# Loading w_out behind the first batch's keys, with the linear product as a third piece and the key work moved back in group 0's turn

## The chip, the cores and the metric

One core of one Trainium2 chip. The metric is the device time of one execution in microseconds (us), taken as the median of several executions. All runs told here are of the fast state. The span in a profile is about 1.8 us shorter than the time of the same execution (in six executions with fillers, told below, 2.0 to 2.5). The mean granted clock of an execution is the share of TensorE's full clock that it got on average, 1.000 being all of it.

## The reference, cut to what matters

Agent attention, then a feed-forward layer that takes the larger of three products:

```python
# q, k, v: (4, 12544, 128); agents: (4, 49, 128); w1, w2, w3: (128, 768); w_out: (768, 128)
a2k = softmax(scale * agents @ k.T);  agent_v = a2k @ v          # over all keys of a batch
q2a = softmax(scale * q @ agents.T);  x = q2a @ agent_v
h = maximum(maximum(x @ w1, x @ w2), x @ w3)
out = h @ w_out
```

The kernel folds `agent_v` into the weights. For each batch it forms G, 49 rows of agents against all weight columns. With w3-w1, w2-w1 and w1 in place of w1, w2, w3, the larger of three becomes w1 plus a second slice against a rectified first one, and the w1 part goes through w_out at once as a linear product of 128 columns ("the linear part", columns C1O to WC of G).

## The kernel before: the parts that matter

Work is queued with a key by `at(key, function, name, needs, ...)`; the keys are sorted, and what still lacks its needs or a PSUM buffer waits and goes as soon as it can. The result is one fixed program per engine. Queries come in 49 groups of 1024 rows. A group has six slices of 128 columns, each a "first" (`u`), a rectification on ScalarE (`a`), a "second" (`v`) and a maximum on VectorE (`x`); slice 3 does both on ScalarE. In the turn of query group s the keys of the next batch are worked off as key tile s. Ahead of group 0 stands a stage for all of batch 0's keys and values.

```python
    def load_weights():                       # queued behind the loads of four key groups
        for t, w in zip(wst, (moe_w1, moe_w2, moe_w3)):
            nc.sync.dma_start(t, w)
        nc.sync.dma_start(wo_st, moe_w_out.rearrange("(f p) d -> p f d", p=P))
    ...
    def prep_weights():                       # in the key stage
        nc.scalar.activation(w1_bf, wst[0], AF.Copy)
        nc.scalar.activation(wo_bf, wo_st, AF.Copy)
    ...
    def prep_linear1():                       # in the key stage, first_key + 43
        t = small_tile("o_ps")
        for f in range(NF):
            nc.tensor.matmul(t[:, :C], w1T[:, f, :], wo_bf[:, f, :], start=(f == 0), stop=(f == NF - 1))
        nc.scalar.activation(wall[:, C1O + C:C1O + 2 * C], t[:, :C], AF.Copy)
    ...
    def keep_busy(times):                     # filler matmuls
        t = small_tile("m_ps")
        for _ in range(times):
            nc.tensor.matmul(t, ident, busy, start=True, stop=True, skip_group_check=True)
```

PSUM holds three large buffers ("uv") and two small ones ("om").

The softmax here doesn't subtract the row's maximum and nothing guards it: scores larger than these inputs give would overflow.

Of the kernel before, what the change touches and what calls it, by code (L numbers as in the profile page):

```python
# [11 lines left out]
AF = mybir.ActivationFunctionType  # L12
# [4 lines left out]
def kernel(  # L17
# [18 lines left out]
    nc = tc.nc  # L36
# [81 lines left out]
    def at(key, fn, name=None, needs=(), ring=None, frees=()):  # L118



        ops.append((key, len(ops), fn, name, needs, ring, frees))
# [53 lines left out]
    wo_st = const.tile([P, NF, C], FP32, name="wo_st")  # L176
# [4 lines left out]
    def load_weights():  # L181
        for t, w in zip(wst, (moe_w1, moe_w2, moe_w3)):
            nc.sync.dma_start(t, w)
        nc.sync.dma_start(wo_st, moe_w_out.rearrange("(f p) d -> p f d", p=P))

    ag_bf = const.tile([A, B, C], BF16, name="ag_bf")
    wo_bf = const.tile([P, NF, C], BF16, name="wo_bf")
# [3 lines left out]
    C21, C31, C1O = 0, Dff, 2 * Dff  # L191
    wall = const.tile([P, 2 * Dff + 3 * C], BF16, name="wall")
    nc.vector.memset(wall[:, C1O:], 0.0)
    WC = 2 * Dff + 2 * C
# [8 lines left out]

    def prep_weights():
        nc.scalar.activation(w1_bf, wst[0], AF.Copy)
        nc.scalar.activation(wo_bf, wo_st, AF.Copy)
        fi = slice(FI * P, (FI + 1) * P)
        nc.vector.tensor_tensor(out=wall[:, C21:C21 + Dff], in0=wst[1], in1=wst[0], op=ALU.subtract)
        nc.vector.tensor_tensor(out=wall[:, C31:C31 + Dff], in0=wst[2], in1=wst[0], op=ALU.subtract)
        nc.vector.tensor_tensor(out=wall[:, C31 + FI * P:C31 + (FI + 1) * P], in0=wst[2][:, fi],  # L210
                                in1=wst[1][:, fi], op=ALU.subtract)

    def prep_linear0():
        t = small_tile("m_ps", BF16)
# [23 lines left out]
    def k_group(b, t0, n, key, s):  # L238
# [3 lines left out]
        K = None if early else table(s)  # L242
# [75 lines left out]
        if early:  # L318
            g = ("early", t0)
            at(key - 30, load)  # L320
            at(key - 5, cast_k)
            at(key - 4, cast_v)
            at(key, turn_k, ("kt", g), (), "uv", [("kt_out", g)])
            at(key + 0.5, evacuate, ("kt_out", g), [("kt", g)])

            last = [("normalise", 0)] if t0 + n == NT else []
            late = max(0, (key - last_key) / 6 + 2)
            at(min(key + 6.6, last_key + 0.58 + 0.02 * late), scores, ("ks", g), [("kt_out", g)],
               "uv", [("ka", g)] + last)
            at(min(key + 7, last_key + 0.64 + 0.01 * late), exps, ("ke", g), [("ks", g)])  # L330
            done = last_key + (0.6 + 0.1 * late if late >= 1 else 0.55)
            at(min(key + 13.2, done), values, ("kv", g), [("ke", g)])
            at(min(key + 13.6, done + 0.01), add_values, ("ka", g), [("kv", g)])
        else:
            at(key - 24.6, load)
            at(max(key - 12.6, last_key - 3.4 + 0.2 * s), cast_k, ("k_cast", s))
            at(max(key - 10.6, last_key - 3.3 + 0.2 * s), cast_v, ("v_cast", s))
            if s > 1:
                at(max(key - 9.1, last_key - 3.2), turn_k, ("kt_out", s), [("k_cast", s)])
            else:  # L340

                turn = 1.2 if s else last_key + 1.05
                at(turn, turn_k, ("kt", s), (), "uv", [("kt_out", s)])
                at(turn + 0.05, evacuate, ("kt_out", s), [("kt", s)])

            at(key + K["ks"] if s else K["u0"] + 0.6, scores, ("ks", s), [("kt_out", s), ("ho", s)])
            at(key + K["ke"], exps, ("ke", s), [("ks", s)])
            at(key + K["ke"] + 1.5, add_exps, ("kx", s), [("ke", s)])
            at(key + K["kv"], values, ("kv", s), [("ke", s), ("v_cast", s)])
            at(key + K["ka"], add_values, ("ka", s), [("kv", s)])  # L350

    def k_tail(b, sum_key, keys, s):
        d = {}

        def reduce():
            d["e"] = work.tile([P, A], FP32, tag="e_sum", name="e_sum")
            nc.vector.tensor_reduce(out=d["e"], in_=Eacc[b].rearrange("p (j a) -> p a j", a=A),
                                    axis=mybir.AxisListType.X, op=ALU.add)

        def total():  # L360
            d["s"] = host[s]
            nc.tensor.matmul(host[s][:, :A], ones, d["e"], start=True, stop=True,
                             skip_group_check=True)

        def normalise():

            r = (last_tile["t"] if s is None else d["s"])[:, :A]
            nc.vector.reciprocal(r, Vacc[b][:, A:] if s is None else r)
            d["avT"] = work.tile([P, H], BF16, tag="avT", name="avT")
            nc.vector.memset(d["avT"][:, A:], 0.0)  # L370
            nc.vector.tensor_tensor(out=d["avT"][:, :A], in0=Vacc[b][:, :A], in1=r, op=ALU.mult)
            G[b] = work.tile([P, WC], BF16, tag="G", name="G")

        def product(c0, c1, on_vector):
            t = uv_tile()
            cuts = [c for c in range(c0, c1, 512)] + [c1]
            for i, (a, z) in enumerate(zip(cuts, cuts[1:])):
                for lo, hi in ((a, min(z, C1O)), (max(a, C1O), z)):
                    for h in range(2 if lo < hi else 0):


                        c = lo + (C if lo >= C1O and h == 0 else 0)
                        nc.tensor.matmul(t[h * H:(h + 1) * H, i, lo - a:hi - a], d["avT"],  # L383
                                         wall[:, c:c + hi - lo], start=True, stop=True,
                                         skip_group_check=True)
            src = t.rearrange("p i c -> p (i c)")[:, :c1 - c0]
            if on_vector:
                nc.vector.tensor_copy(out=G[b][:, c0:c1], in_=src)
            else:
                nc.scalar.activation(G[b][:, c0:c1], src, AF.Copy)  # L390

        if s is not None:
            at(sum_key - 1, reduce, ("sum_e", b), [("kx", s - 1)])
            at(sum_key, total, ("total", s), [("sum_e", b), ("ho", s)])
        at(sum_key + (0.9 if s is None else 0.01), normalise, ("normalise", b),
           [("ka", ("early", NT - last_size)) if s is None else ("total", s)])
        for i, (c0, c1) in enumerate(((C31, WC), (C21, C31))):
            on_vector = s is None and i == 0
            at(keys[i], lambda c0=c0, c1=c1, on_vector=on_vector: product(c0, c1, on_vector),
               ("product", b, i), [("normalise", b)], "uv", [("product", b, i)])  # L400


    def split(t0, t1, step):
# [10 lines left out]
    def q_group(s):  # L414
# [3 lines left out]
        key = 6.0 * s  # L418
# [36 lines left out]
        K = table(s)  # L455
# [63 lines left out]
        def out_linear(o):  # L519
            t = d["o", o] = small_tile("o_ps")  # L520
            for i, jj in enumerate(pairs[o]):
                nc.tensor.matmul(t[:, i * 2 * C:(i + 1) * 2 * C], d["e"][:, jj * P:(jj + 1) * P],  # L522
                                 G[batch[jj]][:, C1O:C1O + 2 * C], start=(i == 0), stop=False,
                                 skip_group_check=True)
# [20 lines left out]
                nc.sync.dma_start(out[r0:r1, :].rearrange("(p j) c -> p j c", j=m), src)  # L545

        new = [("product", tails[s], i) for i in range(2)] if s in tails else []

        def put(name, fn, *needs, ring=None, frees=()):
            at(key + K[name], fn, (name, s), needs, ring, frees)  # L550
# [23 lines left out]
        if s:  # L574
            put("ho", host_tile, ring="om", frees=[("rec", s)] + extra)
        else:
            at(K["u0"] - 0.04, host_tile, ("ho", 0), (), "om", [("rec", 0)] + extra)
        put("sum", sums, ("ex", s), ("ho", s),
            *([("ks", s)] if s in hosting else [("total", s)] if s + 1 in tails else []))
        put("rec", recips, ("sum", s))  # L580
# [10 lines left out]
            put(x, each(max_second), (v, s), (a, s),  # L591
                *([(f"oc{o}{f}", s - 2) for o in range(2)] if s >= 2 else []))
        for o in range(2):
            put(f"lin{o}", lambda o=o: out_linear(o), ("ex", s), *new, ring="om", frees=[(f"sc{o}", s)])
            for f in range(NF):
                put(f"oc{o}{f}", lambda o=o, f=f: out_hidden(o, f), (f"lin{o}", s), (f"x{f}", s))
            put(f"sc{o}", lambda o=o: out_scale(o), ("rec", s),
                *[(f"oc{o}{f}", s) for f in range(NF)], *([("store", s - 3)] if s >= 3 else []))
# [23 lines left out]
    at(first_key - 6.5, load_weights)  # L622
    at(first_key + 30.2, prep_weights)
    at(first_key + 37.1, prep_linear0, "lin_a", (), "om", ["lin_a"])
    at(first_key + 43, prep_linear1, "lin_b", ["lin_a"], "om", ["lin_b"])
    fillers = []
    for g, n in enumerate(first_sizes):
        k_group(0, sum(first_sizes[:g]), n, first_key + 6.0 * g, None)

        if 4 <= g < len(first_sizes) - 5:  # L630
            fillers += [(first_key + 6.0 * g + 0.55, 3), (first_key + 6.0 * g + 1.3, 3)]
    k_tail(0, last_key, (last_key + 0.95, last_key + 1.02), None)
    for key, n in fillers + [(last_key + 0.9, 2), (last_key + 1.1, 2),
                             (KEY["u1"] + 0.61, 2)]:
        at(key, lambda n=n: keep_busy(n), ("busy", key), (), "om", [("busy", key)])
# [45 lines left out]
```

## Time and profile before

| | |
|---|---|
| time, median | 466.05 us (465.85 to 466.12, 3 runs) |
| span of the profiled execution | 465.3 us |
| TensorE, VectorE, ScalarE, GpSimd busy | 94%, 87%, 85%, 36% |
| stage of batch 0's keys | until about 42 us, DMA share 0.98 at 380 GB/s |
| TensorE without a gap | from about 57 us |

The prediction below shows the lines and reads them. One thing about this profile was seen only later: its execution is one of the longer ones. Its time was 467.13 us, 1.1 above the median, and the cast of key tile 0 starts at 44.40 us. In a profile of a kernel that has the same program up to there (`b_keys`, below) it starts at

```profile
43.12 1.15 POOL L252 CAST k_bf<-st 128x1152 bf16<-128x1152 f32 x1 [0.48 <-DMA st<-in_k_dram]
```

and spans of the kernel before in later runs are mostly 464.2 us. A delay of about 1.1 us in the loads of the key stage thus lies in the profile of before and not in the timed runs. So moments are compared below by their distance from the start of key tile 0's cast.

### The profile page before, as it was taken

The page shows a single profiled execution, that of the slowest core. Times are in us where ns is not written, and L with a number is a line of the kernel's source. Part 1 is how long each engine was busy: PE and PEld are TensorE (multiplying, and loading weights), DVE is VectorE, ACT ScalarE, POOL GpSimd, SP SyncE. Part 2 cuts the span into 40 slices and gives each one's busy share as a digit, 9 for nine tenths or more (in the row PEclk, how much of TensorE's full clock was granted, in tenths as well). Part 3 has the DMA queues.
Part 4 walks back from the last instruction along what each step waited for, and adds up shares of the span by engine and source line. Part 5 has one row for each costly group of instructions (what it writes and reads, how often), then busy time and mean ns, then how long its engine had stood idle before and what let it go on. Part 6 is the DMA issues. An engine that isn't in the chain of part 4 may idle for free.

```text
span 465.3 us, 13301 instructions
## 1 busy us (share of the span) xinstructions
PE 436.1 (94%) x5452; PEld 274.3 (59%) x5456; DVE 405.6 (87%) x516; ACT 396.6 (85%) x461; POOL 166.6 (36%) x166
## 2 busy tenths in 40 slices
PE   2496899999999999999999999999999999999996
PEld 2365466666655766666656666666656555555554
DVE  3164699999998999999999999999998989999995
ACT  3366889989989999899889898998999989999992
POOL 2244864553550544535262446353230100100000
PEclk9999999999999999999999999999999999999999
DMA  8999999998998999997997999997746557553222
GB/s 320 394 412 404 409 270 378 298 347 227 297 310 276 279 273 333 314 273 214 271 345 261 279 323 309 275 272 191 176 114 194 147 169 174 160 136 114 69 86 97
DMA packets 82632, 118.53 MB, mean 255 GB/s; under 512 B 56391, under 2 KB 57867, under 8 KB 82571
## 3 DMA queue, kind: packets, MB, share of 16 engines
q1 hardware_dynamic: 82368, 117.59, 83.5%
q8 instruction: 42, 0.69, 0.6%
q14 instruction: 19, 0.16, 0.1%
q10 hardware_dynamic: 203, 0.10, 0.1%
HBM read 78.74 MB, written 25.69 MB: 224 GB/s over the span
## 4 chain that ended last, share of the span: by engine, by line
PE 77%; ACT 6%; issue 3%; DVE 3%; ACTq 0%; DVEq 0%
PE uv_ps L492 33%; PE o_ps L531 28%; PE o_ps L522 5%; ACT a_sb L507 4%; PE m_ps L446 4%; PE m_ps L466 3%; DVE r L517 2%; PE m_ps L295 2%; PE m_ps L284 1%; PE m_ps L480 1%; ACT uv_ps L504 1%; ACT e_q L472 1%; PE uv_ps L383 1%; PE o_ps L613 0%; ACT G L390 0%
## 5 line engine op out<-in xcount | busy, mean ns | idle before, releaser
L517 DVE TENSOR_TENSOR r<-uv_ps,a_sb 128x1024 bf16<-128x1024 f32 x245 | 297.4, 1220 | 15.6 <-PE uv_ps L492 5.9
L507 ACT ACTIVATE a_sb<-uv_ps 128x1024 bf16<-128x1024 f32 x245 | 240.6, 1027 | 13.2 <-PE uv_ps L492 11.7
L492 PE MATMUL uv_ps<-e_q,G 49*128 49x512 bf16 (+3 forms) x1248 | 186.3, 368 | 2.2 <-DVE r L517 0.6
L531 PE MATMUL o_ps<-wo_bf,r 128*128 128x128 bf16 x2352 | 174.7, 220 | 0.2 <-DVE r L517 0.2
L531 PEld LDWEIGHTS <-r 128*128 128x128 bf16 x2352 | 137.8, 98 | 39.8 <-issue 37.9
L492 PEld LDWEIGHTS <-G 49*128 49x128 bf16 x1248 | 57.9, 93 | 63.4 <-issue 31.1
L312 POOL TENSOR_TENSOR Eacc<-Eacc,e_k 128x441 f32<-128x441 f32 (+1 forms) x30 | 30.5, 1016 | 129.8 <-ACT e_k L289 129.8
L538 DVE TENSOR_TENSOR o_sb<-o_ps,recips 128x512 f32<-128x512 f32 x98 | 67.5, 689 | 9.4 <-PE o_ps L531 6.5
L441 POOL CAST q_bf<-st 128x1024 bf16<-128x1024 f32 x49 | 51.0, 1043 | 63.1 <-DMA qT<-q_bf 61.8
L515 ACT ACTIVATE r<-uv_ps 128x1024 bf16<-128x1024 f32 x49 | 50.2, 1024 | 21.8 <-PE uv_ps L492 21.7
L252 POOL CAST k_bf<-st 128x1152 bf16<-128x1152 f32 (+2 forms) x45 | 51.0, 1132 | 28.8 <-DMA st<-in_k_dram 27.1
L504 ACT ACTIVATE uv_ps<-uv_ps 128x1024 f32<-128x1024 f32 x49 | 49.5, 1011 | 1.0 <-ACT a_sb L507 0.7
L522 PE MATMUL o_ps<-G,e_q 128*128 128x256 bf16 x196 | 38.0, 276 | 0.0
L259 POOL CAST v_bf<-st 128x1152 bf16<-128x1152 f32 (+1 forms) x33 | 37.5, 1137 | 0.6 <-DMA st<-in_v_dram 0.3
L472 ACT ACTIVATE e_q<-m_ps 128x512 bf16<-128x512 f32 x49 | 29.8, 609 | 0.5 <-PE m_ps L466 0.5
L257 ACT ACTIVATE v_bf<-st 128x1152 bf16<-128x1152 f32 (+1 forms) x12 | 12.9, 1072 | 16.1 <-DMA st<-in_v_dram 16.1
L272 DVE COPY kT<-uv_ps 128x1152 bf16<-128x1152 bf16 (+1 forms) x14 | 9.9, 708 | 17.5 <-PE uv_ps L266 17.4
L522 PEld LDWEIGHTS <-e_q 128*128 128x128 bf16 x196 | 12.5, 97 | 18.5 <-issue 17.8
L266 PE MATMUL uv_ps<-ident,k_bf 128*128 128x128 bf16 x116 | 11.2, 254 | 12.3 <-POOL k_bf L252 11.8
L446 PEld LDWEIGHTS <-q_bf 128*128 128x128 bf16 x264 | 14.8, 98 | 13.1 <-issue 11.5
L451 DVE COPY qT<-m_ps 128x1024 bf16<-128x1024 bf16 x32 | 21.8, 680 | 0.0
L446 PE MATMUL m_ps<-ident,q_bf 128*128 128x128 bf16 x264 | 20.4, 220 | 0.3 <-POOL q_bf L441 0.3
(68 smaller groups left out, 233.4 us busy)
## 6 DMA issues: line engine op xcount, KB each, us to landing
st<-in_q_dram SPq DMA_DIRECT2D x46, 512.0 KB, 5.3
out_dram<-o_sb SPq DMA_DIRECT2D x46, 512.0 KB, 3.8
st<-in_k_dram SPq DMA_DIRECT2D x40, 576.0 KB, 7.0
st<-in_v_dram SPq DMA_DIRECT2D x40, 576.0 KB, 7.5
st<-in_k_dram SPq DMA_DIRECT2D x3, 512.0 KB, 6.9
st<-in_v_dram SPq DMA_DIRECT2D x3, 512.0 KB, 6.1
wst<-in_moe_w_dram SPq DMA_DIRECT2D x3, 384.0 KB, 10.8
st<-in_q_dram SPq DMA_DIRECT2D x2, 384.0 KB, 4.7
```

The source lines that it names most:

```text
L252: nc.gpsimd.tensor_copy(out=d["kb"][:, :n, :], in_=d["k"][:, :n, :])
L259: nc.gpsimd.tensor_copy(out=d["vb"][:, :n, :], in_=d["v"][:, :n, :])
L441: nc.gpsimd.tensor_copy(out=d["qb"], in_=d["q"])
L446: nc.tensor.transpose(t[:, j * P:(j + 1) * P], d["qb"][:, j, :], ident)
L492: nc.tensor.matmul(t[:, h, j0 * P:j1 * P], G[b][h * H:h * H + A, col + f * P:col + (f + 1) * P], d["e"][h * H:h * H + A, j0 * P:j1 * P], s ...
L504: nc.scalar.activation(u, u, AF.Relu)
L507: nc.scalar.activation(a_sb[f], u, AF.Relu)
L515: nc.scalar.activation(r, v_ps[f], AF.Relu)
L517: nc.vector.tensor_tensor(out=r, in0=v_ps[f], in1=a_sb[f], op=ALU.max)
L522: nc.tensor.matmul(t[:, i * 2 * C:(i + 1) * 2 * C], d["e"][:, jj * P:(jj + 1) * P], G[batch[jj]][:, C1O:C1O + 2 * C], start=(i == 0), stop ...
L531: nc.tensor.matmul(t[:, c:c + C], r_sb[f][:, h, jj * P:(jj + 1) * P], wo_bf[:, f, :], start=False, stop=True, skip_group_check=True)
L538: nc.vector.tensor_tensor(out=d["out"][:, j:j + m, :], in0=d["o", o].rearrange("p (j c) -> p j c", c=C), in1=d["r"][:, j:j + m].unsqueeze( ...
```

## The change

Its intent: w_out isn't needed until the first outputs, so its 393 KB should not hold up the keys that group 0 waits for; the linear part, which needs w_out, then has to follow in group 0's turn; and group 0's own key work, whose tile comes no sooner, moves behind the first slices. Cut to its core:

```diff
     def load_weights():
         for t, w in zip(wst, (moe_w1, moe_w2, moe_w3)):
             nc.sync.dma_start(t, w)
+
+    def load_w_out():
         nc.sync.dma_start(wo_st, ...)
...
         nc.scalar.activation(w1_bf, wst[0], AF.Copy)
-        nc.scalar.activation(wo_bf, wo_st, AF.Copy)
...
+    def prep_w_out():
+        nc.gpsimd.tensor_copy(out=wo_bf, in_=wo_st)
...
-            at(key + K["ks"] if s else K["u0"] + 0.6, scores, ...)
+            at(key + K["ks"] if s else 0.26, scores, ...)
...
-        for i, (c0, c1) in enumerate(((C31, WC), (C21, C31))):
+        pieces = ((C31, C1O), (C21, C31), (C1O, WC)) if s is None else ((C31, WC), (C21, C31))
+        for i, (c0, c1) in enumerate(pieces):
...
-            at(K["u0"] - 0.04, host_tile, ("ho", 0), ...)
+            at(0.25, host_tile, ("ho", 0), ...)
...
-    at(first_key + 43, prep_linear1, "lin_b", ["lin_a"], "om", ["lin_b"])
+    at(last_key - 29.85, load_w_out)
+    at(last_key - 3.28, prep_w_out)
+    at(1.9, prep_linear1, "lin_b", ["lin_a"], "om", ["lin_b"])
...
-    k_tail(0, last_key, (last_key + 0.95, last_key + 1.02), None)
+    k_tail(0, last_key, (last_key + 0.95, last_key + 1.02, 2.4), None)
```

More of the change, by code (lines that the diff above doesn't have):

```diff
@@ L344, in k_group @@
                 at(turn + 0.05, evacuate, ("kt_out", s), [("kt", s)])
-            at(key + K["ks"] if s else K["u0"] + 0.6, scores, ("ks", s), [("kt_out", s), ("ho", s)])
+            at(key + K["ks"] if s else 0.26, scores, ("ks", s), [("kt_out", s), ("ho", s)])
             at(key + K["ke"], exps, ("ke", s), [("ks", s)])
@@ L396, in k_tail @@
            [("ka", ("early", NT - last_size)) if s is None else ("total", s)])
-        for i, (c0, c1) in enumerate(((C31, WC), (C21, C31))):
+        pieces = ((C31, C1O), (C21, C31), (C1O, WC)) if s is None else ((C31, WC), (C21, C31))
+        for i, (c0, c1) in enumerate(pieces):
             on_vector = s is None and i == 0
             at(keys[i], lambda c0=c0, c1=c1, on_vector=on_vector: product(c0, c1, on_vector),
-               ("product", b, i), [("normalise", b)], "uv", [("product", b, i)])
+               ("product", b, i), [("normalise", b)] + ["lin_b"] * (i == 2), "uv", [("product", b, i)])
     def split(t0, t1, step):
@@ L547, in q_group @@
         new = [("product", tails[s], i) for i in range(2)] if s in tails else []
+        new_linear = new if s else [("product", 0, 2)]
         def put(name, fn, *needs, ring=None, frees=()):
@@ L576, in q_group @@
         else:
-            at(K["u0"] - 0.04, host_tile, ("ho", 0), (), "om", [("rec", 0)] + extra)
+            at(0.25, host_tile, ("ho", 0), (), "om", [("rec", 0)] + extra)
         put("sum", sums, ("ex", s), ("ho", s),
@@ L593, in q_group @@
         for o in range(2):
-            put(f"lin{o}", lambda o=o: out_linear(o), ("ex", s), *new, ring="om", frees=[(f"sc{o}", s)])
+            put(f"lin{o}", lambda o=o: out_linear(o), ("ex", s), *new_linear, ring="om",
+                frees=[(f"sc{o}", s)])
             for f in range(NF):
```

## The prediction

> **What bounds the kernel now.** I read the page first, then busy time by stretches, then the chain of waits, then what GpSimd (POOL) and ScalarE (ACT) did between 42 and 57 us.
>
> ```profile
> PE 436.1 (94%) x5452; PEld 274.3 (59%) x5456; DVE 405.6 (87%) x516; ACT 396.6 (85%) x461; POOL 166.6 (36%) x166
> ```
> TensorE is busy for 94% of the span, so the question is where the missing 6% lies. The stretches answer it.
>
> ```profile
> 0.00:42.00 42.00, 22.70 (x386) 18.91 (x389) 16.21 (x37) 20.24 (x26) 13.98 (x18) 1.00 0.98 380
> 42.00:47.40 5.40, 4.79 (x76) 3.02 (x74) 3.46 (x9) 3.05 (x6) 3.74 (x4) 1.00 1.02 408
> 47.40:53.90 6.50, 5.07 (x60) 2.83 (x61) 3.57 (x7) 4.38 (x7) 5.24 (x6) 1.00 1.02 409
> 53.90:57.30 3.40, 3.18 (x27) 1.12 (x26) 2.80 (x3) 3.40 (x6) 3.02 (x4) 1.00 1.03 410
> ...
> 65.60:132.00 66.40, 66.40 (x860) 42.28 (x860) 63.66 (x81) 60.63 (x72) 31.10 (x30) 1.00 1.05 309
> ```
> Columns: stretch, length, busy us of PE, weight load, DVE, ACT, POOL, then granted clock, DMA share, GB/s. Until 42 us the core waits for batch 0's keys and values: DMA is full at about 410 GB/s. From 57 us on PE has no gap. So the change can act only on the start, up to about 57 us; every microsecond that PE's dense run begins sooner or later comes out at the end almost 1:1, because nothing behind it has slack.
>
> GpSimd casts what lands, in order:
> ```profile
> 42.88 1.04 POOL L441 CAST q_bf<-st 128x1024 bf16<-128x1024 f32 x1 [1.25 <-DMA st<-in_q_dram]
> 44.40 1.15 POOL L252 CAST k_bf<-st 128x1152 bf16<-128x1152 f32 x1 [0.49 <-DMA st<-in_k_dram]
> 45.81 1.15 POOL L259 CAST v_bf<-st 128x1152 bf16<-128x1152 f32 x1 [0.26 <-PE uv_ps L383]
> 47.00 1.04 POOL L441 CAST q_bf<-st 128x1024 bf16<-128x1024 f32 x1
> 48.50 1.15 POOL L252 CAST k_bf<-st 128x1152 bf16<-128x1152 f32 x1 [0.46 <-DMA st<-in_k_dram]
> ```
> These are group 0's queries, group 0's keys and values, group 1's queries and keys. Between 44 and 48 us GpSimd has nearly no room: query tile 1 is cast the moment value tile 0 is done.
>
> ScalarE in group 0's turn:
> ```profile
> 46.64 0.80 ACT L390 ACTIVATE G<-uv_ps 128x768 bf16<-128x768 f32 x1
> 47.84 1.02 ACT L507 ACTIVATE a_sb<-uv_ps 128x1024 bf16<-128x1024 f32 x1 [0.39 <-PE uv_ps L492]
> 48.76 0.54 ACT L289 ACTIVATE e_k<-m_ps 128x441 bf16<-128x441 f32 x1
> 49.18 1.03 ACT L507 ACTIVATE a_sb<-uv_ps 128x1024 bf16<-128x1024 f32 x1
> 50.88 1.01 ACT L504 ACTIVATE uv_ps<-uv_ps 128x1024 f32<-128x1024 f32 x1 [0.67 <-ACT a_sb L507]
> 52.94 1.02 ACT L515 ACTIVATE r<-uv_ps 128x1024 bf16<-128x1024 f32 x1 [1.05 <-PE uv_ps L492]
> 53.86 1.98 ACT L507 ACTIVATE a_sb<-uv_ps 128x1024 bf16<-128x1024 f32 x2
> ```
> I call these G1, a0, key exps, a1, relu of slice 3, second relu of slice 3, then a2 and a4. The gaps of 0.67 and 1.05 us are waits for slices. The chain of waits runs through the last two:
> ```profile
> 53.86 1.99 ACT a_sb L507 x2
> 55.85 0.04 issue
> 55.90 0.39 PE uv_ps L492 x2
> 56.29 0.32 PE o_ps L613
> ```
> From 55.90 on the chain is PE after PE. So the hand-over from "ACT sets the pace" to "PE sets the pace" is the end of a4 at 55.85 us. That is the point to compute after the change.
>
> [...] PE idles 1.00 us at 48.35 before the key values' product (it waits for the key exps) although slices 0 and 3, next in program order, need nothing from it. So order in the program is what this change trades in. [...] ScalarE here shows 278 ns for 128 columns and 1027 for 1024, so about 0.84 ns a column and 0.17 us fixed. Cutting one evacuation into two is therefore paid for.
>
> **The change part by part.**
>
> *w_out's load moves behind query tile 0.* 768x128 floats are 393 KB, at 410 GB/s 0.96 us. Batch 0's keys, its values from the fifth group on, and query tile 0 land 0.96 us sooner. All that comes behind (key tile 0 and later) has the same bytes ahead of it as before, so it lands when it did: key tile 0 still at 44.40.
>
> *Product in three pieces.* The first evacuation on DVE, 1024 columns in 1.23 us, becomes 768 columns, about 0.95; two matmuls fewer ahead. Slices can start from the first two pieces; query tile 0's exps (46.15 to 46.75 before, now 0.96 sooner) and G1 (now 45.7 to 46.5) are ready in time.
>
> *Start of the slices.* The transposes of key tile 0 stand ahead of slice 0 on PE. They started at 46.37, after PE's earlier work, with slice 0 1.04 us later at 47.41. Now they wait for the cast that ends at 44.40 + 1.15 = 45.55, so they start at 45.60 and slice 0 at 46.64. Gain 0.77, not 0.96. a0 then runs 47.07 to 48.09.
>
> *w_out's cast on GpSimd.* 1152 columns take 1.15 and 512 take 0.62 us, so 768 take about 0.83. By its key it comes between value tile 0 and query tile 1: 47.00 to 47.83. Query tile 1's cast moves to 47.85 to 48.90 (before 47.00 to 48.04).
>
> *Key work behind the first slices.* New PE order: slices 0, 1, two fillers, second slice 0, slice 3, then query tile 1's transposes (key 0.222), then key tile 0's scores (0.26). The second slice 0 and slice 3 are done by 48.4 (slice 3 needs a0's buffer, 48.09). But query tile 1's transposes stand ahead of the scores and now wait until 48.95; they take 0.46, so scores start at 49.41 (before 47.95). Key exps still stand ahead of a1 on ACT: they run at 49.9 (before 48.76), ACT idling from 48.09 to 49.9. Then a1 ends at 51.3 (before 50.2) and slice 3's first relu at 52.25 (before 51.9; it loses less because its slice is ready and the gap of 0.67 is gone). On PE the key values' product follows the exps at 50.5 and the sums at 50.7; reciprocals and the first maximum follow at about 51.25 to 51.5 on DVE (before 50.97). Then second slices 1 and 3 run about 52.5 to 53.05, against 52.24 to 52.86. So this reordering eats the 0.77 gained and about 0.2 more.
>
> *Linear part in group 0's turn.* Its two parts had cost nothing on the path in the DMA stage:
> ```profile
> L206 ACT ACTIVATE wo_bf<-wo_st 128x768 bf16<-128x768 f32 x1 | 0.8, 827 | 0.0
> ...
> L223 ACT ACTIVATE wall<-o_ps 128x128 bf16<-128x128 f32 x1 | 0.3, 278 | 0.9 <-PE o_ps L222 0.9
> ```
> Now six matmuls (key 1.9) follow second slice 3 on PE, 53.05 to 53.4, and their evacuation of 0.28 us stands on ACT ahead of slice 3's second relu (key 2.4). From first matmul to evacuation took 0.53 before, so it starts at 53.58 and the relu at 53.75 (before 52.94, +0.8). The third piece needs a PSUM buffer of the three; the only one that comes free there is slice 3's, when that relu ends (54.75). So: relu ends, two matmuls of 256 columns and their drain (about 0.5), evacuation of 256 columns on ACT (0.17 + 256 x 0.84 ns = 0.38, of which 0.3 before the next may start), then a2. That is a2 at about 55.55 against 53.86; a4 ends at about 57.5 against 55.85.
>
> Sum at the hand-over: start of slices -0.77; key work and the cast ahead of it +1.0; wait for the linear product and its evacuation +0.55; buffer wait and evacuation of the third piece +0.85; total +1.6. Later stages are unchanged in work, so 466.05 + 1.6 = 467.7. I take 467.5, since some of the waits in a row may overlap more than I allow.
>
> **The rivals.**
> First: the gain of the load is kept. If query tile 1's transposes don't hold up the scores, or the third piece takes a buffer free earlier, ACT needs only 0.28 + 0.3 more, which fits the old 1.05 gap. Then the hand-over comes up to 0.8 earlier: about 465.3. For it: slices 0 and 3 are moved ahead of a wait that PE spent idle, a sensible aim. Against it: in-order queues and a GpSimd queue full from 44 to 48 us.
> Second: all of it is hidden, because DMA at 410 GB/s sets when later keys land and the start just waits elsewhere: 466.0. Against: after 57.3 us nothing on PE waits for a DMA.
> Third: the delay is larger, the fillers and slices behind the third piece on PE waiting too, and DVE starved after: 468.5.
>
> **Range and chances.** All branches lie within 0.7% of 466; 2% would be 9.3 us, more than the whole stretch from 42 to 57 us can lose or give (PE idles about 2.3 us in it). Predicted 467.5, range 465.3 to 468.6. Chances: faster 0.01, same 0.98, slower 0.01.
>
> **What would show each step.** Query tile 0's cast near 41.9 and the first slice near 46.6: the load's gain. A cast of 768 columns on GpSimd at 47.0, query tile 1's cast ending near 48.9, key scores near 49.4: the reordering's loss. ACT idle for over 1 us ahead of the key exps; slice 3's second relu at 53.7 instead of 52.9; an evacuation of 256 columns between it and a2, a2 at 55.5. PE dense from about 57.6. I am wrong if the key exps come before 49 us, if a2 starts before 54, or if the span shrinks.

## The result, and the profile after

469.72 us median (468.43 to 470.68, 6 runs) against 466.05 (465.85 to 466.26, 6 runs): 3.7 us slower, ratio 1.0078 with a 95% interval of 1.0063 to 1.0093. Ratios are the mean time of one kernel's fast runs over that of the other's of the same rounds, so not quite the ratio of the medians quoted. It is still within 2%, but above the predicted range of 465.3 to 468.6. Two things stand out in the list of runs. The spread is 2.2 us where that of before is 0.4. And the mean granted TensorE clocks are 0.989 to 0.996, where before has 0.998 to 1.000 in nearly all. By estimate from the fall in the profile below (0.50 for 3.4 us), one such stretch takes 3.4 x 0.5 / 466 = 0.0037 off the mean, so 0.996 is about one such stretch and 0.993 two. (Every profile here also shows the clock fall once after the last matmul, where no matmul is left to slow: to 0.50 at 463.92 us in the profile of before, whose last matmul ends at 461.00. The mean from 430 us on is 0.95 to 0.99 in all of them; 0.998 and 1.000 differ by that.) The profile below is of the fastest of the six (span 466.6, clock 0.996).

The stretches of the changed kernel, columns as in the prediction:

```profile
0.00:42.00 42.00, 25.18 (x429) 20.62 (x430) 17.69 (x42) 20.30 (x26) 14.53 (x19) 1.00 0.98 381
42.00:47.40 5.40, 4.71 (x36) 1.66 (x33) 2.25 (x5) 3.35 (x4) 3.83 (x4) 1.00 1.02 407
47.40:53.90 6.50, 4.88 (x55) 3.10 (x53) 3.71 (x6) 2.52 (x4) 5.84 (x7) 0.74 1.02 408
53.90:57.30 3.40, 2.94 (x19) 0.90 (x18) 1.23 (x2) 3.40 (x6) 2.57 (x3) 1.00 1.02 410
...
65.60:132.00 66.40, 66.36 (x864) 42.44 (x861) 63.56 (x81) 60.60 (x73) 31.05 (x30) 1.00 1.05 289
```

From 65 us on TensorE is as busy as before. In group 0's turn, 47.4 to 53.9 us, ScalarE does 2.52 us of work instead of 4.38, and the granted clock is 0.74 instead of 1.00.

GpSimd, in order of time:

```profile
40.44 1.04 POOL L447 CAST q_bf<-st 128x1024 bf16<-128x1024 f32 x1 [1.27 <-DMA st<-in_q_dram]
43.28 1.15 POOL L256 CAST k_bf<-st 128x1152 bf16<-128x1152 f32 x1 [1.80 <-DMA st<-in_k_dram]
44.71 1.15 POOL L263 CAST v_bf<-st 128x1152 bf16<-128x1152 f32 x1 [0.29 <-DMA st<-in_v_dram]
45.80 0.83 POOL L215 CAST wo_bf<-wo_st 128x768 bf16<-128x768 f32 x1
46.58 1.04 POOL L447 CAST q_bf<-st 128x1024 bf16<-128x1024 f32 x1
```

Query tile 0 now comes 2.84 us ahead of key tile 0 (before: 1.52), and w_out's cast of 0.83 us stands ahead of query tile 1's. TensorE behind it:

```profile
47.67 0.62 PE L452 MATMUL m_ps<-ident,q_bf 128*128 128x128 bf16 x8 [0.25 <-POOL q_bf L447]
48.13 0.39 PE L288 MATMUL m_ps<-agT,kT 128*128 128x49 bf16 x9
49.21 0.39 PE L299 MATMUL m_ps<-e_k,v_bf 128*128 128x49 bf16 x9 [0.69 <-ACT e_k L293]
...
52.92 0.80 PE L226 MATMUL o_ps<-wo_bf,w1T 128*128 128x128 bf16 x6 [0.23 <-DVE qT L457]
```

Key tile 0's scores (second line) wait behind query tile 1's transposes, which wait for the cast. The last line is the linear product: it waits for VectorE's evacuation of query tile 1 (`qT`). ScalarE:

```profile
45.95 1.02 ACT L513 ACTIVATE a_sb<-uv_ps 128x1024 bf16<-128x1024 f32 x1 [0.95 <-PE uv_ps L498]
48.62 0.54 ACT L293 ACTIVATE e_k<-m_ps 128x441 bf16<-128x441 f32 x1 [1.64 <-PE m_ps L288]
49.05 1.02 ACT L513 ACTIVATE a_sb<-uv_ps 128x1024 bf16<-128x1024 f32 x1
49.95 1.03 ACT L510 ACTIVATE uv_ps<-uv_ps 128x1024 f32<-128x1024 f32 x1
53.75 0.28 ACT L227 ACTIVATE wall<-o_ps 128x128 bf16<-128x128 f32 x1 [2.77 <-PE o_ps L226]
53.92 1.02 ACT L521 ACTIVATE r<-uv_ps 128x1024 bf16<-128x1024 f32 x1
54.83 0.39 ACT L394 ACTIVATE G<-uv_ps 128x256 bf16<-128x256 f32 x1
55.09 1.96 ACT L513 ACTIVATE a_sb<-uv_ps 128x1024 bf16<-128x1024 f32 x2
```

Two new waits: 1.64 us ahead of the key exps, 2.77 us ahead of the linear evacuation (the place of the old 1.05). The chain of waits hands over from ScalarE to TensorE where it did before, at the end of a4:

```profile
55.22 1.84 ACT a_sb L513 x2
57.06 0.04 issue
57.10 0.39 PE uv_ps L498 x2
57.50 0.32 PE o_ps L621
```

From key tile 0's cast to this point it is 57.06 - 43.28 = 13.78 us; before it was 55.85 - 44.40 = 11.45. The difference, 2.3 us, is the difference of the spans, 466.6 against the usual 464.2. So all the loss of this execution lies in group 0's turn, as predicted. But this was the fastest run, and the median lies 1.3 us higher. The clock is the candidate for that. Busy time and clock of the changed kernel ahead of and in the fall:

```profile
47.00:50.40 3.40, 1.99 (x36) 1.54 (x36) 0.21 (x3) 1.78 (x3) 3.21 (x4) 0.97 1.03 414
50.40:53.80 3.40, 3.16 (x20) 1.61 (x18) 3.40 (x5) 0.63 (x2) 2.94 (x4) 0.53 1.03 408
```

TensorE is 1.99 / 3.40 = 59% busy, then its clock is 0.50 for 3.4 us (from 50.2 to 53.6).

### The profile page after: what moved, and what is told of

The parts are those of the page before. It is cut to its first block, busy times and chain, and to the rows that moved or that the text cites. A ratio compares the mean times of both kernels' runs of the same rounds, so it can differ in the third digit from the quotient of the medians.

```text
span 466.6 us, 13305 instructions
## 1 busy us (share of the span) xinstructions
PE 439.6 (94%) x5456; PEld 275.1 (59%) x5456; DVE 405.3 (87%) x516; ACT 396.3 (85%) x461; POOL 166.6 (36%) x167
## 4 chain that ended last, share of the span: by engine, by line
PE 78%; DMA 9%; ACT 6%; issue 3%; DVE 2%; SPq 1%; POOL 1%; ACTq 0%; POOLq 0%; DVEq 0%
PE uv_ps L498 33%; PE o_ps L537 28%; DMA st<-in_v_dram 7%; PE o_ps L528 5%; ACT a_sb L513 4%; PE m_ps L452 4%; PE m_ps L472 3%; DMA st<-in_k_dram 2%; DVE r L523 2%; PE m_ps L288 1%; PE m_ps L299 1%; ACT uv_ps L510 1%; PE m_ps L486 1%; SPq L251 1%; ACT e_q L478 1%
```

## The experiments

Theory "order": the loss is the order in which engines come to their work, as predicted. Theory "clock": the fall of TensorE's clock adds to it. Rival "load": the later load and cast of w_out delay something behind. In all there were 16 runs, two of them of a kernel that had run already (`a_again`, `a_warm_b`); all gave correct results. "Before" in the same rounds was 465.97 to 466.21 us.

| run | what it is | us, median | vs. before | mean clocks of its runs |
|---|---|---|---|---|
| a_again | the changed kernel again | 469.69 | +3.7 | 0.991 to 0.998 |
| a_oldkeys | changed, key work in its old place | 466.81 | +0.8 | 0.994 to 1.000 |
| b_keys | before, key work moved alone | 467.00 | +1.0 | 0.998 to 1.000 |
| b_third | before, linear part moved alone | 467.56 | +1.6 | 0.999 to 1.000 |
| b_piece | before, third piece moved alone | 466.62 | +0.65 | 0.998 to 1.000 |
| b_both | before, key work and linear part moved | 470.04 | +4.0 | 0.993 to 1.000 |
| a_warm, a_warm_b | changed, gaps filled | 468.70, 468.33 | +2.5, +2.3 | 0.992 to 0.999 |
| a_warm2, a_warm3 | changed, more gaps filled | 468.80, 468.55 | +2.8, +2.5 | 0.991 to 1.000 |
| a_qfirst | changed, w_out's cast later | 469.61 | +3.4 | 0.993 to 0.996 |
| a_dve | changed, linear part on VectorE | 468.24 | +2.2 | 0.988 to 0.998 |
| a_mend, a_mend2 | a_oldkeys, linear part on VectorE | 466.27, 466.71 | +0.1, +0.7 | 0.994 to 1.000 |
| b_cold, b_colder | before with fewer fillers | 465.55, 465.38 | -0.7, -0.6 | 0.993 to 1.000 |

### The changed kernel again

> The changed kernel unchanged, for more runs and a second profile. Its six runs lay at 468.4 to 470.7 us with mean clocks 0.996 to 0.989. If a fall of the granted clock in group 0's turn is part of the loss, the profile again has a stretch near half clock somewhere between 45 and 60 us and the slower runs have the lower mean clocks; median 469.5. If order alone makes the loss, the clock of the runs and their times don't go together.

469.69 us (468.09 to 470.90). One of the six runs kept a mean clock of 0.998, and it is the fastest: 468.09 us, span 466.3. The other five have 0.991 to 0.996 and take 469.6 to 470.9. The second profile (span 468.4):

```profile
50.00:54.00 4.00, 2.38 (x20) 1.48 (x20) 3.65 (x6) 1.22 (x3) 3.51 (x5) 0.78 1.02 406
54.00:58.00 4.00, 3.76 (x14) 0.89 (x14) 0.15 (x1) 2.80 (x5) 2.62 (x3) 0.50 1.02 411
58.00:62.00 4.00, 4.00 (x38) 1.61 (x39) 3.67 (x3) 3.70 (x6) 1.25 (x2) 0.87 1.23 261
```

The clock is at half from 52.2 to 59.0 us, twice as long as in the first profile, and now the fall lies over the hand-over to TensorE. So the same program takes 466.3 without a fall (by its mean clock), 466.6 with 3.4 us of it early in the turn, and 468.4 with 6.8 us of it: the fall costs from 0.3 to 2.1 us by where it lies and how long it lasts. The order alone costs 468.1 - 466.0 = 2.1 us.

### Each part alone

Undo the key work's move in the changed kernel:

```diff
-            at(key + K["ks"] if s else 0.26, scores, ...)
+            at(key + K["ks"] if s else K["u0"] + 0.6, scores, ...)
-            at(0.25, host_tile, ("ho", 0), ...)
+            at(K["u0"] - 0.04, host_tile, ("ho", 0), ...)
```

> The changed kernel with the key work of group 0 back ahead of its second slices. Order theory: key exps come right behind the first relu (under 0.2 us of ACT idle instead of 1.64), about 1 us is won back, 467.0 to 468. Clock theory: PE idles less, the clock stays at 0.998, and the spread of the runs falls below 0.5 us; 466.5. If the later load and cast of w_out are the cause, it stays at 469.5.

466.81 us (466.63 to 466.93): 2.9 us won back, more than the order theory alone had said, and the spread is gone. The key exps stand right behind a0; the wait for the linear product stays:

```profile
46.94 0.54 ACT L293 ACTIVATE e_k<-m_ps 128x441 bf16<-128x441 f32 x1
...
52.22 0.28 ACT L227 ACTIVATE wall<-o_ps 128x128 bf16<-128x128 f32 x1 [2.15 <-PE o_ps L226]
```

The load theory falls: load and cast are still late here. The reverse edit in the kernel before (`b_keys`):

> The kernel before with only the key work of group 0 moved behind the first slices. Order theory: ACT idles ahead of the key exps for about 1 us, 466.8 to 467.3 with the clock at 0.998. Clock theory: a dip in the profile near 50 us and runs with mean clocks below 0.996, 467.5 to 469. If the load is the cause: 466.0.

467.00 us (466.89 to 467.18), +1.0, no low clock: as the order theory had it. Next, the linear part alone, w_out loaded and cast early:

```diff
+        pieces = ((C31, C1O), (C21, C31), (C1O, WC)) if s is None else ((C31, WC), (C21, C31))
-    at(first_key + 43, prep_linear1, ...)
+    at(1.9, prep_linear1, ...)
-    k_tail(0, last_key, (last_key + 0.95, last_key + 1.02), None)
+    k_tail(0, last_key, (last_key + 0.95, last_key + 1.02, 2.4), None)
```

> The kernel before (w_out loaded and cast early, keys in the old order) with only the linear product and the third piece in group 0's turn. Order theory: two more ACT evacuations and a wait for the linear product ahead of a2, 466.9 to 467.5. Clock theory: PE idles little more than before, clock 0.998, spread below 0.5 us. If the load is the cause: 466.0.

467.56 us, a little above the range: +1.6, clock 0.999 or more. The spread is 1.1 us where under 0.5 was expected: one of the five executions took 468.53 us at a clock of 0.999, so about 1 us can come without a fall, as in the profile of before. It differs from `a_oldkeys` only by the load and the cast, so these are worth 467.56 - 466.81 = 0.75 us, the 0.77 of the prediction. To split the linear part, only the third piece moved; the linear product (`prep_linear1`) back at `first_key + 43`:

> The kernel before with the third piece alone as a piece of its own in group 0's turn; the linear product and its evacuation stay in the stage of batch 0's keys. Order theory: ScalarE no longer waits for the linear product ahead of slice 3's second relu; left is one evacuation of 256 columns (0.27 us from start to start) ahead of a2, less what the smaller first piece gives: 466.1 to 466.4. If the third piece itself (its buffer, its two matmuls) made the 1.5 us: 467.3 to 467.6.

466.62 us, above the 466.1 to 466.4 expected. ScalarE in this run and then in `b_third`, from slice 3's second relu (L516 in both) on:

```profile
52.66 1.02 ACT L516 ACTIVATE r<-uv_ps 128x1024 bf16<-128x1024 f32 x1 [1.04 <-PE uv_ps L493]
54.07 0.38 ACT L390 ACTIVATE G<-uv_ps 128x256 bf16<-128x256 f32 x1 [0.39 <-PE uv_ps L383]
```

```profile
52.91 0.28 ACT L223 ACTIVATE wall<-o_ps 128x128 bf16<-128x128 f32 x1 [2.14 <-PE o_ps L222]
53.09 1.02 ACT L516 ACTIVATE r<-uv_ps 128x1024 bf16<-128x1024 f32 x1
53.99 0.39 ACT L390 ACTIVATE G<-uv_ps 128x256 bf16<-128x256 f32 x1
```

Without the linear product the wait ahead of the relu is 1.04 us, as in the kernel before, but the piece itself waits 0.39: its matmuls start at 53.73, when the relu has ended (52.66 + 1.02). So of the 1.6 us the linear product's wait makes 467.56 - 466.62 = 0.9, the third piece 0.65.

### Key work and linear part together

Both edits in the kernel before, w_out early:

> The kernel before, w_out loaded and cast early, with both the key work behind the first slices and the linear part in group 0's turn. Order theory: the costs of the two alone, 1.0 and 1.5, add up: 468.5 if the clock holds. Clock theory, if these two together make TensorE idle enough: runs with a mean clock of 0.996 or less and a spread over 1 us, median 469 to 470.5. If the fall needs the load's shift as well, all runs lie within 0.5 us.

470.04 us. Two runs kept the clock (0.998 and 1.000): 468.30 and 468.58 us. That is the sum of the two alone, 466.0 + 1.0 + 1.6 = 468.6. Four runs had 0.993 to 0.995: 469.9 to 470.4 us. Its profile:

```profile
46.00:50.00 4.00, 3.27 (x41) 1.56 (x40) 0.76 (x1) 2.29 (x4) 3.23 (x3) 1.00 1.02 410
50.00:54.00 4.00, 2.24 (x28) 1.53 (x25) 3.30 (x6) 1.49 (x2) 3.51 (x5) 0.93 1.02 406
54.00:58.00 4.00, 4.00 (x19) 0.95 (x17) 0.67 (x2) 2.94 (x5) 2.55 (x3) 0.64 1.04 416
```

So the fall needs neither the later load nor GpSimd's cast. It came where two waits stand close together in one turn (1.64 and 2.77 us on ScalarE in the first profile of the changed kernel); each of them alone left the clock up in all of its five executions.

### Filling the gaps

The changed kernel with matmuls in TensorE's gaps that wait for nothing new and change no result: they write second slice 0 again.

```diff
+        def again(times):
+            for _ in range(times):
+                for h in range(2):
+                    nc.tensor.matmul(v_ps[0][:, h, :], G[0][h * H:h * H + A, C21:C21 + P],
+                                     d["e"][h * H:h * H + A, :], start=True, stop=True, ...)
+        if s == 0:
+            for key0, n0 in ((0.2, 1), (0.261, 2), (0.3, 1)):
+                at(key0, lambda n0=n0: again(n0), ("again", key0), [("v0", 0)])
```

(The key values' product moves to key 0.262, the sums stay behind it. This takes no wait away: in the profile a4 ends 13.66 us after the start of key tile 0's cast, in the changed kernel 13.78.)

> The changed kernel with eight more matmuls in TensorE's gaps of group 0's turn, which write second slice 0 again with the same values (two ahead of query tile 1's transposes, four ahead of the key values' product, two behind the sums). They add TensorE work and take no wait away. Clock theory: the granted clock stays at 1.00, mean 0.998 or more, the spread falls below 0.5 us, and the time falls to what order alone costs, about 467.8 (467.3 to 468.3). If order alone explained all 3.7 us, or if the time's growth came from something else, more work leaves it at 469.5 or above.

468.70 us (468.08 to 469.73). More work on TensorE made the kernel 1.0 us faster, so order alone does not explain the 3.7. But three of five runs still had 0.992 or 0.993, and one of those took 469.73. The profile, a run with 0.999:

```profile
46.00:50.00 4.00, 3.59 (x46) 1.72 (x44) 0.00 (x0) 2.18 (x3) 3.86 (x4) 1.00 1.02 411
50.00:54.00 4.00, 2.42 (x24) 1.41 (x23) 3.72 (x6) 1.54 (x4) 3.51 (x5) 1.00 1.03 407
54.00:58.00 4.00, 3.62 (x30) 1.28 (x28) 1.92 (x3) 4.00 (x6) 2.56 (x3) 1.00 1.02 408
```

Between 50 and 54 us TensorE is still only 60% busy. Five fillers more there (`for key in (1.3, 1.305, 1.31, 1.85, 1.86): at(key, fill, None, [("fill", 0)])`):

> The changed kernel with the eight repeated matmuls of the last try and five fillers more in the two gaps of TensorE that stayed (between key tile 1's transposes and second slice 1, and ahead of the linear product), where that try's profile was still only a third busy. Clock theory: no run below 0.997, spread under 0.5 us, median at the level of the unthrottled runs of the changed kernel, 468.1 (467.9 to 468.4). If the clock isn't what makes the spread: 469.5, spread above 1.5 us.

468.80 us (468.29 to 469.32): missed. Two of the five runs had 0.994 and 0.996, the spread is 1.0 us, and the median is not below the first set's. Two fillers more ahead of key tile 0's transposes (`(last_key + 1.03, 2)`):

> The second set of fillers with two more ahead of key tile 0's transposes, where TensorE waits 0.5 us for the cast. Clock theory: clock 1.00 between 40 and 60 us, all spans within 0.8 us of each other (the start of the key stage varies by that much in the kernel before too), 466.4 to 467.2, median time 468.2 to 468.9. If a fall isn't behind the slow runs: spans up to 469 stay.

468.55 us (468.20 to 469.38): the median is as expected, the spans of 466.0 to 467.5 lie wider than the 0.8 us, and one run had 0.991. And the first set looked at again:

> The first set of fillers again, for a second profile. Its spans were 466.3 to 467.7. If the profile shows the clock at 1.00 from 40 to 60 us, the span is 466.3 to 467.1; a span of 467.5 or more goes with a stretch of clock below 0.95 there.

468.33 us (468.00 to 469.08), clock 1.00 from 40 to 62 us in the profile, span 466.5. In all four profiles of filled kernels the clock stays at 1.00 from 40.1 us to 62 us, and no span of their 20 runs is above 467.7, where 9 of the 12 runs of the changed kernel are at 467.8 or more. The fillers hold the clock there and take away 0.9 to 1.4 of the 1.6 us between the median and the unthrottled run.

The traces put what is left ahead of group 0's turn and behind the span. From the start of key tile 0's cast to the end of the span the four profiles take 422.95 to 423.14 us. For the changed kernel without a fall it is 423.0, by an estimate (span 466.3, the cast taken at 43.3 as in its profiles). So fall and fillers cost nothing there. But that cast starts at 43.18, 43.54, 43.66 or 44.15 us, and six of the 20 runs end 2.0 to 2.5 us above their span instead of 1.8; the cause of neither is known. `a_warm2`'s profile, the latest of the four, has a fall in the key stage, from 36.6 to 40.0 us. `a_mend` (below) has one too, from 35.6 to 39.0 us:

```profile
12.00:40.00 28.00, 20.85 (x347) 17.21 (x350) 11.89 (x22) 15.41 (x20) 9.33 (x10) 0.94 1.03 402
```

Its key tile 0 is cast at 43.21 us all the same, and its 466.00 us, at a mean clock of 0.994, is among its shortest times. `b_piece`'s profile has that cast at 44.14 us and no fall. So such a fall needn't delay the cast, nor a late cast come from a fall, and a low mean clock alone doesn't say that time was lost: it matters where the fall lies.

### The cast's place

```diff
-    at(last_key - 3.28, prep_w_out)
+    at(last_key - 3.24, prep_w_out)      # behind query tile 1's cast
```

> The changed kernel with the cast of w_out behind query tile 1's cast on GpSimd instead of ahead of it. Order theory: query tile 1's transposes and with them key tile 0's scores and exps come up to 0.75 us sooner, so the order's cost falls by 0.5 to 0.8 us; the linear product still finds w_out cast. With the clock still falling in some runs: 468 to 469.3; if the shorter gap also keeps the clock up: 467.0 to 467.5. If the cast's place didn't matter: 469.7.

469.61 us, no gain in the median: the key exps come at 48.31 instead of 48.62, a third of a microsecond sooner where up to 0.75 was expected, and the clock fell in the profile for 6.8 us. Its only run at 0.996 took 467.63. So w_out's cast is a small term of the order.

### The linear part on VectorE

```diff
-        nc.scalar.activation(wall[:, C1O + C:C1O + 2 * C], t[:, :C], AF.Copy)
+        nc.vector.tensor_copy(out=wall[:, C1O + C:C1O + 2 * C], in_=t[:, :C])
-            on_vector = s is None and i == 0
+            on_vector = s is None and i != 1
-    at(1.9, prep_linear1, ...)               # third piece at 2.4
+    at(2.54, prep_linear1, ...)              # third piece at 2.6
```

With the key work as changed:

> The changed kernel (load and key work as changed) with the linear part evacuated on VectorE behind its second maximum. Order theory: 1.0 for the key work, 0.35 for the cast of w_out ahead of it, less 0.75 of the load, and the linear part nearly free as in the version with the old key order: 466.6 to 467.3 if the clock holds. If the key work with the load's shift is what lets the clock fall, a low clock shows in the profile between 48 and 60 us and the median is 468 or above.

468.24 us (467.34 to 469.40), above the expected range. The two runs at 0.998 took 467.34 and 467.63; the four at 0.988 to 0.996 took 468.16 to 469.40. The profile was one of the unthrottled (span 465.8). With the key work in its old place:

> The changed load kept, with the key work in its old place and both evacuations of the linear part (the product's and the third piece's) on VectorE, behind its second maximum, where it idles for about 2 us. Order theory: ScalarE doesn't wait for the linear product, a2 starts right behind slice 3's second relu, the 1.5 us of the linear part go and the 0.75 us of the load remain: 465.2 to 465.6, clock 0.998 or more. If the cost of the linear part were its TensorE work or its GpSimd cast, it stays at 466.8.

Missed: 466.27 us, level with before (ratio 0.9999). The wait for the linear product is gone from ScalarE, but a new one stands ahead of a4, the last line:

```profile
50.97 1.02 ACT L521 ACTIVATE r<-uv_ps 128x1024 bf16<-128x1024 f32 x1 [1.03 <-PE uv_ps L498]
51.90 1.02 ACT L513 ACTIVATE a_sb<-uv_ps 128x1024 bf16<-128x1024 f32 x1
53.85 1.02 ACT L513 ACTIVATE a_sb<-uv_ps 128x1024 bf16<-128x1024 f32 x1 [0.94 <-PE uv_ps L498]
```

Slice 4 now stands on TensorE behind the third piece, which waits for VectorE. So the third piece went behind slice 4 and second slice 2 (key 3.36):

> The last version with the linear part on VectorE, its third piece now behind slice 4 and second slice 2 on TensorE instead of ahead of them. In the last version a4 waited 0.94 us for slice 4, which stood behind the third piece's wait for the linear evacuation. Order theory: that wait goes, 465.2 to 465.8. If the load's gain is used up by the added work on TensorE and VectorE as such, it stays at 466.2.

Missed: 466.71 us, though two runs took 465.93 and 465.97. (Before has two levels in this round as well, seven runs at 465.9 to 466.0 and two at 466.5 and 466.6, so the 0.7 us need not belong to this version.) The wait ahead of a4 shrank to 0.28 us, and the load's 0.75 us still did not show at the end. With the linear part's matmuls and two evacuations in a turn where TensorE, VectorE and ScalarE are 91%, 87% and 80% busy (49 to 56 us in its profile), I found no place for them that costs less than the load gives.

### Fewer fillers in the kernel before

The six fillers of the last keys and of group 0's turn removed (`b_cold`), then five more in group 0's turn (`b_colder`):

```diff
-    for key, n in fillers + [(last_key + 0.9, 2), (last_key + 1.1, 2),
-                             (KEY["u1"] + 0.61, 2)]:
+    for key, n in fillers:
```

> The kernel before without the last six filler matmuls (two each at the end of batch 0's keys and in group 0's turn), the other way round: less TensorE work, all else alike. Clock theory: in some or all runs the granted clock falls between 44 and 58 us, the mean is below 0.997 in those, and they take 1 us or more longer; the spread grows beyond 1 us. Without it: the time stays at 466.0 or falls by up to 0.5 us.

465.55 us; five runs at 0.999 or 1.000 took 465.3 to 465.7, the sixth fell to 0.993 and took 467.43.

> The kernel before without its last six fillers, as tried, and without five more of the ramp's fillers in group 0's turn. Clock theory: more runs than one in six fall to a mean clock of 0.996 or below, and those take 1.5 to 3 us longer than its unthrottled runs, which lie at 465.3 to 465.6 as there is no other change on the path. Without it: all runs 465.0 to 465.6.

465.38 us (465.15 to 465.98), all five at 0.998: a miss for the clock theory's expectation. So less filling does not by itself bring the fall in most runs; in the order of before no 3.4 us from 43.5 us on are under 68% busy in the profiles of either. Where the sixth run of `b_cold` fell isn't known: it has no profile. This version is the only one that beats both kernels, by 0.13% (0.9987, interval 0.9974 to 0.9999), by shorter work on TensorE and at the risk that `b_cold` showed in one run of six.

## Why the prediction was wrong

The place of the loss was right, and so were the first four moments below, to 0.2 us. Distances from the start of key tile 0's cast, in us (before: 44.40, predicted on the same 44.40, after: 43.28):

| moment | before | predicted | after |
|---|---|---|---|
| slice 0 | 3.01 | 2.24 | 2.24 |
| end of query tile 1's cast | 3.64 | 4.50 | 4.34 |
| key exps | 4.36 | 5.50 | 5.34 |
| first maximum on VectorE | 6.57 | 6.9 to 7.1 | 7.11 |
| linear evacuation | - | 9.18 | 10.47 |
| a2 | 9.46 | 11.15 | 11.81 |
| hand-over, end of a4 | 11.45 | 13.1 | 13.78 |

(Before: 47.41; 47.00 + 1.04; 48.76; 50.97; 53.86; 55.85. After: 45.52; 46.58 + 1.04; 48.62; 50.39; 53.75; 55.09; 57.06.)

- The load's gain of 0.77 at slice 0: right, and measured as 0.75 us in the pair `b_third` and `a_oldkeys`. "Key work and the cast ahead of it +1.0": right in size (`b_keys`, +1.0), but `b_keys` has no cast in the way; `a_qfirst` puts the cast's share of the key exps' delay at 0.3.
- "Wait for the linear product and its evacuation +0.55" was mis-sized. I let the six matmuls follow second slice 3 at once. In the trace they wait for VectorE's evacuation of query tile 1, whose small PSUM buffer they take; VectorE comes to it only after the first maximum and key tile 1. The evacuation stood 1.3 us later than predicted, about 0.3 of it from the low clock of that run (0.83 us from the first matmul to the evacuation, 0.54 in `b_third`). Alone, the wait for the product costs 0.9 us (`b_third` less `b_piece`).
- "Buffer wait and evacuation of the third piece +0.85" had the wrong buffer for the changed kernel. I said that the only one free was slice 3's, so that the matmuls would follow the second relu. They ran at 54.18, when VectorE's second maximum had ended (52.78 + 1.21) and before the relu ended at 54.94, and the evacuation followed the relu with no wait. From the relu's start to a2 it is 1.17 us instead of 1.8. In `b_piece`, where the relu ends before that maximum (53.68 against 54.30), the piece did wait for the relu, as I had said, and ScalarE idled 0.39 us for it. By the runs the piece costs 0.65.
- Sum of the order: predicted +1.6, measured +2.1, at 468.1 us inside the range. That is one execution without a fall, but the four profiles with fillers agree: from key tile 0's cast to the end they take 2.0 to 2.2 us more than before's 420.90. The parts alone give -0.75 + 1.0 + 1.6 = 1.85; the rest may be w_out's cast.
- The step that failed is the one that the sum lacks: "Later stages are unchanged in work, so 466.05 + 1.6". It took TensorE's clock as constant, in group 0's turn and at the hand-over as well as later. The new waits left TensorE 49% to 59% busy for 3.4 us of group 0's turn, in three profiles; in 11 of the 12 runs the mean clock was 0.996 or less, and the median lies 1.6 us above the one run that had 0.998. 2.1 + 1.6 = 3.7, the measured loss. The fillers of the kernel before, which I counted only as work, were the hint.

The rivals: the gain of the load was not kept, and nothing was hidden by the DMA. The third, a larger delay with the cause in VectorE and fillers, had the right sign, and VectorE did idle for 2.17 us ahead of 56.17 (before: 0.55), but the fall was not in it. The signs listed in the prediction, shifted by the 1.12 us of the earlier key tile 0, came as said except that the second relu and a2 stand 1.3 and 0.7 us later; read without the shift, "key exps before 49 us" (48.62) would have called the reordering's loss wrong. A sign for the clock was not among them.

That the fall follows from the idle time rests on three things: the 3.4 us ahead of it, a stretch as long as one fall, are 49% to 59% busy in three profiles (59% in the first profile of the changed kernel, 1.74 / 3.40 = 51% in the second, 1.66 / 3.40 = 49% in `b_both`), each part alone kept the clock in its five runs, and filling the gaps keeps it (1.00 from 40.1 to 62 us in four profiles). Not settled is how much idle time it takes. The stretches ahead of the fall in `a_again` and `b_both`, and one of `b_keys`, which had no fall:

```profile
48.80:52.20 3.40, 1.74 (x27) 1.15 (x26) 1.85 (x4) 2.33 (x3) 2.76 (x4) 1.00 1.03 411
50.20:53.60 3.40, 1.66 (x17) 1.01 (x17) 2.90 (x6) 1.28 (x2) 2.93 (x4) 0.98 1.02 407
49.00:52.40 3.40, 1.80 (x27) 1.15 (x26) 1.92 (x4) 2.27 (x3) 2.90 (x3) 1.00 1.03 409
```

Slid along in steps of 0.2 us, the most idle 3.4 us of `b_keys` (from 48.6) are 1.60 us busy, 47%, and those of `a_again` and `b_both` are no lower. So the busy share of such a stretch doesn't decide alone: `b_keys` at 47% and `a_warm` at 1.97 / 3.40 = 58% (from 50.0 us) had no fall, and the first profile of the changed kernel had one behind 59%, with no gap of TensorE above 0.7 us between 46.6 and 50.2 us. What else decides was not shown, and whether the key work alone would bring a fall in other executions is open. In slices of 0.2 us of four profiles with a fall the clock reads 1.00 or 0.50, and values between stand only in the slices in which a fall starts or ends; the falls ahead of the last matmul, in six profiles, last 3.4 us (`after`: 3.413, from 50.174 to 53.587 us) or 6.8.

One warning on the clock's column: it reads 1.00 from the start, but in the profiles of before and after nine transposes of a key tile take 1.14 us up to about 21 to 24 us, near the 1.10 in the fall at 50.12 us of the first profile of the changed kernel, and 0.66 to 0.68 later. So the clock was most likely at half there too, in both kernels alike, by an estimate from these times.

## What to carry to other kernels

Moving w_out's load out of the DMA-bound stage gained 0.75 us here, of the 0.96 that its 393 KB take at 410 GB/s, but the work that needs it moved along, from a stage where engines wait for data into one where they are the bound: 0.75 us gained against 1.0 and 1.6 lost. An instruction moved in an engine's order must be followed to the buffer it will take and to the engine that frees it: here the linear product waited for VectorE, and its evacuation stood 1.3 us later than predicted. And a wait on TensorE was not only its own length here: where two came close together the clock fell to 0.50 for 3.4 or 6.8 us in four profiles, at a cost of 0.3 to 2.1 us. So read the clock of every run, where in the profile it falls, and the spread of the times, not the time alone.
